# Moving five groups of SBUF tiles to different start bytes modulo 512 in a TensorE-bound kernel

## The chip, the core and the metric

The kernel runs on one core of a Trainium2 chip. The time is the device time of one execution in microseconds (us), the median of three runs.

## What is computed

A decaying (retention-like) attention over 2 batches, 8 heads, 768 positions and head size 64 gives 1536 tokens of 512 features. Two feed-forward layers follow, and they are most of the work:

```python
def _moe_ref(x, w_in, w_out):            # 512 -> 2048 -> 512
    h = x @ w_in
    g = np.where(h >= 1, h, np.where(h <= -1, 0.0, (h + 1) ** 2 / 4))
    return g @ w_out
def _moe2_ref(x, w_gate, w_val, w_out):  # 512 -> 1536 -> 512
    gate = 1.0 / (1.0 + np.exp(-(x @ w_gate)))
    return (gate * (x @ w_val)) @ w_out
```

The weights arrive as 64-bit floats, all else in 32 bits.

## The kernel before

Every large product is made of single-pass matmuls (type `float32r`) on a high and a low part of each operand: high times high, low times high and high times low, summed in PSUM. A matmul has a stationary operand of 128 by 128, which a weight load (LDWEIGHTS, row PEld of the profile) puts into the array, and a moving operand of 128 by 512, which is then streamed past it. Each matmul has its own weight load. All of this is on TensorE, in the order in which the code issues it.

- Up to some 66 us the attention runs, in small fp32 matmuls, with the first products of the first layer between them.
- `hidden` (lines 211 to 213) multiplies a slice of weights `w` (stationary) by the tokens `xh`, `xl` (moving), 12 matmuls per call. It serves the whole first layer and a third of the second.
- `project` (line 265) is the second product of each layer, 12 matmuls per call. In the first layer the weights are stationary and the activations `gh`, `gl` moving; in the second layer the activations are stationary and the weights moving. (The trace lists the operands of line 265 with the moving one first.)
- `product` (line 387), called seven times by `pair` with 6 matmuls each, serves two thirds of the second layer's first products by a scheme with fewer multiplications: the stationary operand is `w` or a sum or difference of weights (the "forms", tiles `s`), the moving one is `xh`, `xl` or a sum or difference of tokens (the "token forms", `xth`, `xtl`).

VectorE (DVE), ScalarE (ACT) and GpSimd (POOL) convert the weights to high and low parts (lines 99 to 120), apply the activation functions and add finished PSUM sums into `part` (line 287). The DMA queue of SyncE brings the weights.

The tiles of a pool lie one behind the other in each partition of SBUF, each rounded up to 32 bytes, and the pools follow each other in the order in which they are opened: `wp` (weights), `rawp`, `tp`, `xp` (tokens), `gp` (activations), `acp` (`half` and `part0`), then `late` (`part1`, `part2`, token forms) and `fp` (forms). The tiles of these pools are multiples of 512 bytes, except `half`, one number of 4 bytes. A stationary slice is 512 bytes of a partition and begins at a multiple of 512 bytes within its tile, and a moving operand is 2048 bytes and does so too. So all operands of one group have the same start byte modulo 512.

Of the kernel before, what the change touches and what calls it, by code (L numbers as in the profile page):

```python
# [7 lines left out]
F32 = mybir.dt.float32  # L8
# [9 lines left out]
P = 128  # L18
# [21 lines left out]
def fused_kernel(ctx: ExitStack, tc: tile.TileContext, qkv, qd, cst, w1, w2, out):  # L40
# [3 lines left out]
    wp = ctx.enter_context(tc.tile_pool(name="wp", bufs=NWP))  # L44
    rawp = ctx.enter_context(tc.tile_pool(name="rawp", bufs=NRAW))
    tp = ctx.enter_context(tc.tile_pool(name="tp", bufs=2))
    xp = ctx.enter_context(tc.tile_pool(name="xp", bufs=1))
    psx = ctx.enter_context(ExitStack())
    banks = {None: psx.enter_context(tc.tile_pool(name="ps", bufs=8, space=PSUM))}
    gp = ctx.enter_context(tc.tile_pool(name="gp", bufs=4))  # L50
    acp = ctx.enter_context(tc.tile_pool(name="acp", bufs=1))

# [161 lines left out]
        return h  # L214


    half = acp.tile([P, 1], F32, name="half")
    part = {0: acp.tile([P, 4, 512], F32, name="part0")}
    seq = []
    n0 = 0  # L220
# [597 lines left out]


    late = ctx.enter_context(tc.tile_pool(name="late", bufs=1, reuse_waits="tile"))  # L820
    fp = ctx.enter_context(tc.tile_pool(name="fp", bufs=4, reuse_waits="tile"))
    for t in range(1, NTT):
        part[t] = late.tile([P, 4, 512], F32, name=f"part{t}")
# [72 lines left out]
```

## Time and profile before

| | |
|---|---|
| median of three runs | 612.15 us |
| the three runs | 609.75, 612.15, 612.18 us |
| span of the profiled execution, first to last instruction | 608.4 us |
| median less span (what lies around it) | 3.75 us |
| PE busy | 596.9 us, 98% of the span |
| PEld, DVE, ACT, POOL busy | 80%, 71%, 53%, 18% |

Matmuls are pipelined: one begins before the one before it has left the array, so the duration of a row and the distance between two starts (called the pitch below) are two numbers. A busy share of 98% says only that matmuls follow each other without gaps.

### The profile page before, as it was taken

To read this page: it belongs to the slowest core of one execution; us is meant where nothing else is said; L and a number is where in the kernel's file an instruction comes from. 1 tells how busy PE (TensorE), PEld (TensorE's weight loads), DVE (VectorE), ACT (ScalarE), POOL (GpSimd) and SP (SyncE) were. 2 spreads that over 40 slices of the span, in tenths; PEclk is the share of its full clock that TensorE was granted. 3 is DMA by queue.
4 is the path that set the end of the run, shared out by engine and by line. 5 is a ranking of instruction groups with operands and counts; after the bars stand their busy time and mean duration, and the time that the engine had idled before them with its cause. 6 is when DMAs were issued, how large, how long until landed. Compare 5 with 4: busy or idle time off the path is not lost.

```text
span 608.4 us, 7945 instructions
## 1 busy us (share of the span) xinstructions
PE 596.9 (98%) x3016; PEld 487.4 (80%) x3016; DVE 429.4 (71%) x701; ACT 323.1 (53%) x585; POOL 110.9 (18%) x116
## 2 busy tenths in 40 slices
PE   7999999999999999999989999999999999999997
PEld 4887888888888888888868888878888888878885
DVE  7788853677587477467685887699697698594444
ACT  6798663675465466366563556555554554441220
POOL 4379500000000000000000231351241141150000
PEclk9999999999999999999999999999999999999999
DMA  8993420123122022123120223213123123000013
GB/s 298 397 330 132 139 69 2 71 103 103 36 79 95 0 90 85 34 70 103 36 69 0 70 70 103 70 52 123 34 70 103 36 69 105 0 1 0 1 69 138
DMA packets 15813, 52.58 MB, mean 86 GB/s; under 512 B 1688, under 2 KB 2976, under 8 KB 15776
## 3 DMA queue, kind: packets, MB, share of 16 engines
q1 hardware_dynamic: 15760, 52.08, 24.8%
q8 instruction: 23, 0.38, 0.3%
q14 instruction: 14, 0.11, 0.1%
q10 hardware_dynamic: 16, 0.01, 0.0%
HBM read 48.92 MB, written 3.15 MB: 86 GB/s over the span
## 4 chain that ended last, share of the span: by engine, by line
PE 87%; DVE 5%; DMA 4%; ACT 1%; issue 1%; POOL 1%; SPq 0%; DVEq 0%; ACTq 0%; POOLq 0%
PE a L265 35%; PE p L387 15%; PE h L211 11%; PE h L212 11%; PE h L213 11%; DMA u<-in_qkv 2%; DMA raw<-in_w 2%; PE x L748 1%; PE s L666 1%; PE x L739 1%; DVE wr L110 1%; DVE w L120 1%; DVE part L287 1%; DVE gl L433 1%; POOL wr L135 1%
## 5 line engine op out<-in xcount | busy, mean ns | idle before, releaser
L211 PE MATMUL h<-xh,w 128*128 128x512 f32 x320 | 125.9, 393 | 2.2 <-DVE part L287 2.2
L212 PE MATMUL h<-xh,w 128*128 128x512 f32 x320 | 125.2, 391 | 0.0
L213 PE MATMUL h<-xl,w 128*128 128x512 f32 x320 | 125.0, 391 | 0.0
L265 PE MATMUL a<-gh,w 128*128 128x512 f32 x384 | 118.5, 390 | 0.0
L265 PE MATMUL a<-w,gh 128*128 128x512 f32 x288 | 89.0, 390 | 0.1
L246 DVE SCALAR_TENSOR_TENSOR r<-r,h 128x512 f32<-128x512 f32 x48 | 33.0, 687 | 75.1 <-ACT r L242 75.1
L265 PEld LDWEIGHTS a<-gh,w 128*128 128x128 f32 x384 | 72.0, 188 | 15.1 <-POOL w L120 0.3
L241 ACT ACTIVATE r<-h,half 128x512 f32<-128x512 f32 x48 | 33.1, 689 | 89.5 <-PE h L213 89.5
L135 POOL TENSOR_TENSOR wr<-wr 128x256 f32<-128x256 f32 x20 | 16.9, 845 | 347.7 <-DVE w L120 346.9
L287 DVE TENSOR_TENSOR part<-part,a 128x512 f32<-128x512 f32 x108 | 68.1, 681 | 10.2 <-PE a L265 10.2
L265 PE MATMUL a<-gl,w 128*128 128x512 f32 x192 | 74.8, 390 | 0.5 <-DVE gl L234 0.5
L211 PEld LDWEIGHTS h<-xh,w 128*128 128x128 f32 x320 | 60.4, 189 | 15.6 <-DVE part L287 2.7
L213 PEld LDWEIGHTS h<-xl,w 128*128 128x128 f32 x320 | 60.3, 189 | 12.7
L212 PEld LDWEIGHTS h<-xh,w 128*128 128x128 f32 x320 | 60.5, 189 | 12.5
L265 PEld LDWEIGHTS a<-w,gh 128*128 128x128 f32 x288 | 54.0, 188 | 12.0 <-DVE part L287 0.6
L265 PE MATMUL a<-w,gl 128*128 128x512 f32 x144 | 56.6, 393 | 0.4 <-DVE gl L433 0.4
L110 DVE SCALAR_TENSOR_TENSOR wr<-raw,wr 128x512 uint32<-128x512 uint32 x68 | 51.5, 758 | 2.3
L116 ACT ACTIVATE w<-wr 128x512 fp32r<-128x512 f32 x68 | 42.3, 622 | 17.8 <-DVE wr L112 14.9
L233 ACT ACTIVATE gh<-r 128x512 fp32r<-128x512 f32 x64 | 40.0, 625 | 20.9 <-DVE r L246 11.5
L120 DVE TENSOR_TENSOR w<-wr,w 128x512 fp32r<-128x512 f32 x61 | 48.9, 801 | 1.8 <-ACT w L116 1.8
L234 DVE TENSOR_TENSOR gl<-r,gh 128x512 fp32r<-128x512 f32 x64 | 44.6, 696 | 7.7 <-ACT gh L233 7.7
L112 DVE CUSTOM_DVE_ANT_0 wr<-wr,wc 128x1024 uint16<-128x1024 uint16 x60 | 45.2, 753 | 2.7
(92 smaller groups left out, 877.0 us busy)
## 6 DMA issues: line engine op xcount, KB each, us to landing
raw<-in_w SPq DMA_DIRECT2D x68, 512.0 KB, 3.5
u<-in_qkv SPq DMA_DIRECT2D x12, 768.0 KB, 8.2
u<-in_qkv SPq DMA_DIRECT2D x8, 384.0 KB, 5.7
out<-part SPq DMA_DIRECT2D x12, 256.0 KB, 2.0
DT<-pd SPq DMA_DIRECT2D x1, 256.0 KB, 6.5
qp<-pd SPq DMA_DIRECT2D x2, 96.0 KB, 4.4
DT<-pd SPq DMA_DIRECT2D x1, 128.0 KB
cs<-in_cst SPq DMA_DIRECT2D x1, 98.0 KB, 1.9
```

Source lines behind the costliest of these rows:

```text
L110: dve.scalar_tensor_tensor(out=ru, in0=hi, scalar=0x80000000, in1=ru, op0=ALU.bitwise_and, op1=ALU.bitwise_or)
L112: eng.tensor_tensor(out=ri, in0=ri, in1=c, op=ALU.add)
L116: act.activation(ws[i][:, 0], tmps[i][1], AF.Copy)
L120: eng.tensor_tensor(out=ws[i][:, 1], in0=r, in1=ws[i][:, 0].bitcast(F32), op=ALU.subtract)
L211: pe.matmul(h, lhsT=wh, rhs=xh[:, k, tt], start=(k == 0), stop=False)
L212: pe.matmul(h, lhsT=wl, rhs=xh[:, k, tt], start=False, stop=False)
L213: pe.matmul(h, lhsT=wh, rhs=xl[:, k, tt], start=False, stop=(k == NP - 1))
L233: act.activation(gh, g, AF.Copy)
L234: dve.tensor_tensor(out=gl, in0=g, in1=gh.bitcast(F32), op=ALU.subtract)
L265: pe.matmul(accs[j], lhsT=a, rhs=b_, start=(first and m == 0), stop=(last and m == 2))
L287: dve.tensor_tensor(out=o, in0=o, in1=accs[j], op=ALU.add)
L387: pe.matmul(o, lhsT=a, rhs=b_, start=(start and k == 0 and m == 0), stop=(k == HK - 1 and m == 2), skip_group_check=True)
```

## The change

Four paddings are put into the order of the pools. Three are pools with one tile that nobody writes or reads (64, 64 and 416 bytes); the fourth is a wider tile for `half`, 288 bytes instead of 4, of which the same one number is used. No instruction is added, removed or moved; only addresses change.

```diff
+    def shift(name, n):
+        pool_ = ctx.enter_context(tc.tile_pool(name=name, bufs=1))
+        pool_.tile([P, n // 4], F32, name=f"{name}_")
+
+    shift("shx", 64)
     xp = ctx.enter_context(tc.tile_pool(name="xp", bufs=1))
...
+    shift("shg", 64)
     gp = ctx.enter_context(tc.tile_pool(name="gp", bufs=4))
...
-    half = acp.tile([P, 1], F32, name="half")
+    half = acp.tile([P, 72], F32, name="half")[:, 0:1]
...
     late = ctx.enter_context(tc.tile_pool(name="late", bufs=1, reuse_waits="tile"))
+    shift("shf", 416)
     fp = ctx.enter_context(tc.tile_pool(name="fp", bufs=4, reuse_waits="tile"))
```

Start bytes modulo 512, counted from those of the weights:

| group | before | after |
|---|---|---|
| weights `w` | 0 | 0 |
| tokens `xh`, `xl` | 0 | 64 |
| activations `gh`, `gl` | 0 | 128 |
| token forms `xth`, `xtl` | 32 | 416 |
| forms `s` | 32 | 320 |

Distance of the moving operand's start byte from the stationary operand's, modulo 512:

| product | matmuls | before | after |
|---|---|---|---|
| tokens on weights, lines 211 to 213 | 960 | 0 | 64 |
| activations on weights, line 265, first layer | 576 | 0 | 128 |
| weights on activations, line 265, second layer | 432 | 0 | 384 |
| tokens on weights, line 387 | 120 | 0 | 64 |
| token forms on forms, line 387 | 120 | 0 | 96 |
| tokens on forms, line 387 | 120 | 480 | 256 |
| token forms on weights, line 387 | 60 | 32 | 416 |

## Rows read from the trace of the kernel before

**Rows 1.** The page: busy time of the engines, and slices of the span.
```profile
PE 596.9 (98%) x3016; PEld 487.4 (80%) x3016; DVE 429.4 (71%) x701; ACT 323.1 (53%) x585; POOL 110.9 (18%) x116
...
PE   7999999999999999999989999999999999999997
...
PEclk9999999999999999999999999999999999999999
```

**Rows 2.** The chain that ended last: start us, us, engine, tile, line, instructions.
```profile
406.04 5.44 PE a L265 x24
411.48 6.88 PE p L387 x30
...
423.81 9.70 PE p L387 x42
```

**Rows 3.** Timeline of PE, first layer: start us, us, line, operands, instructions merged.
```profile
200.04 0.62 PE L265 MATMUL a<-gh,w 128*128 128x512 f32 x2
...
202.08 0.39 PE L211 MATMUL h<-xh,w 128*128 128x512 f32 x1
```

**Rows 4.** Timeline of PE, second layer, products on forms.
```profile
377.66 0.63 PE L387 MATMUL p<-xh,s 128*128 128x512 f32 x2
...
379.06 0.62 PE L387 MATMUL p<-xh,w 128*128 128x512 f32 x2
```

**Rows 5.** Matmuls of line 387 by operands: duration ns, lowest/median/highest.
```profile
L387 PE MATMUL p<-xh,w x80: 387/389/395, 363.9 to 569.8; 128*128 128x512 f32 x80
...
L387 PE MATMUL p<-xth,s x80: 387/389/398, 366.7 to 572.5; 128*128 128x512 f32 x80
...
L387 PE MATMUL p<-xh,s x80: 392/396/404, 369.4 to 579.4; 128*128 128x512 f32 x80
...
L387 PE MATMUL p<-xl,s x40: 395/396/397, 369.9 to 579.7; 128*128 128x512 f32 x40
...
L387 PE MATMUL p<-xth,w x40: 393/395/399, 376.3 to 578.0; 128*128 128x512 f32 x40
...
L387 PE MATMUL p<-xtl,w x20: 389/393/397, 376.7 to 578.3; 128*128 128x512 f32 x20
```

**Rows 6.** Groups of PE's instructions by form: count, busy us, mean ns, idle before.
```profile
L211 PE MATMUL h<-xh,w 128*128 128x512 f32 x320 | 125.9, 393 | 2.2 <-DVE part L287 2.2
...
L265 PE MATMUL a<-gh,w 128*128 128x512 f32 x384 | 118.5, 390 | 0.0
L265 PE MATMUL a<-w,gh 128*128 128x512 f32 x288 | 89.0, 390 | 0.1
L265 PE MATMUL a<-gl,w 128*128 128x512 f32 x192 | 74.8, 390 | 0.5 <-DVE gl L234 0.5
L265 PE MATMUL a<-w,gl 128*128 128x512 f32 x144 | 56.6, 393 | 0.4 <-DVE gl L433 0.4
```

**Rows 7.** Stages: us, busy us (instructions) of PE, PEld, DVE, ACT, POOL, granted clock, DMA.
```profile
319.00:322.00 3.00, 3.00 (x8) 2.32 (x9) 2.96 (x4) 0.00 (x0) 0.00 (x0) 0.50 0.00 1
...
400.00:450.00 50.00, 50.00 (x220) 40.85 (x219) 42.80 (x63) 27.09 (x49) 16.88 (x17) 1.00 0.23 74
```

**Rows 8.** Timeline of PE around the low clock.
```profile
318.80 0.79 PE L211 MATMUL h<-xh,w 128*128 128x512 f32 x1 [2.24 <-DVE part L287]
319.40 0.63 PE L212 MATMUL h<-xh,w 128*128 128x512 f32 x1
...
321.96 0.42 PE L212 MATMUL h<-xh,w 128*128 128x512 f32 x1
322.21 0.39 PE L213 MATMUL h<-xl,w 128*128 128x512 f32 x1
322.44 0.39 PE L211 MATMUL h<-xh,w 128*128 128x512 f32 x1
...
323.59 0.39 PE L213 MATMUL h<-xl,w 128*128 128x512 f32 x1
```

**Rows 9.** Timeline of the weight loads in the same place.
```profile
322.21 0.19 PEld L211 LDWEIGHTS h<-xh,w 128*128 128x128 f32 x1
322.44 0.19 PEld L212 LDWEIGHTS h<-xh,w 128*128 128x128 f32 x1
```

## The prediction

> **What bounds the kernel now.** The page comes first [rows 1]. PE is busy for 98% of the span, nearly every slice shows a 9, and the granted clock is full in all 40. The other engines stand between 18% and 71%. So 596.9 of 608.4 us pass with one matmul behind the other, and only two things can move the time: how many matmuls there are, which doesn't change, and the pitch, the distance from one start to the next. The busy share can't tell the pitch, for overlapping matmuls are busy all the time however far apart they start; so I read the pitch from the chain and the timeline.
>
> The chain that ended last has stretches of PE alone [rows 2]: 24 matmuls of line 265 in 5.44 us are 226.7 ns each. The timeline of the first layer has nine matmuls from 200.04 to 202.08 us, again 226.7 ns [rows 3]. All of these have operands that start at the same byte modulo 512 (distance 0 in the table above).
>
> The second place to look is line 387, the only line where two distances occur before the change. Its 42 matmuls at 423.81 us take 9.70 us [rows 2]. By the order of the code these are the last two products of one pair and the first five of the next: 24 with distance 0 and 18 with operands 32 bytes apart. If the 24 take 226.7 ns, 4.26 us are left for the 18, which is 236.7 ns, 10.0 more. The 30 at 411.48 us (24 at 0, six at 32) leave 1.44 us for the six, 13.3 ns more each. Alone, six matmuls of tokens on forms go from 377.66 to 379.06 us, 233.3 ns each, 6.6 more [rows 4]; the difference to 10.0 is what their neighbours lose behind them. The durations say the same by operands [rows 5]: medians of 389 ns for tokens on weights and for high token forms on forms (both at 0), 396 and 396 for tokens on forms, 395 and 393 for token forms on weights (all 32 apart). The same line, instruction and shape, with another start byte, is about 6.5 ns longer. So start bytes do matter here, and nearly 2400 matmuls carry them.
>
> Third, is there anything to gain? Around 320 us PE ran at a granted clock of 0.50, its lower level of 1.2 GHz, after 2.24 us of idleness before a matmul that waited for VectorE [rows 7, 8]. From 319.40 to 321.96 us six matmuls have a pitch of 426.7 ns. That is 512 columns at 1.2 GHz, with nothing on top. At 2.4 GHz the same would be 213.3 ns, but 226.7 is what the rows show. So 13.3 ns of each matmul are no streaming of columns. They appear only when the moving operand is read at its full rate, while the weight load of the next matmul is read beside it: at 322.21 us the load for the matmul of 322.44 starts in the same moment as the matmul before it [rows 8, 9]. I read the 13.3 ns as the two reads of SBUF getting into each other's way, and the 32-byte rows as the same thing at another distance.
>
> **The change part by part.** Nothing is issued, waited for or moved; queues, DMAs and waits stay as they are, and the paddings, 800 bytes per partition in all, are never written. The wider `half` is read through the same one column. So the whole change is the price of seven new distances: 64, 96, 128, 256, 384 and 416 instead of 0, 32 and 480.
>
> The counts come from the code and the groups agree with them [rows 5, 6]: 960 matmuls in `hidden`, 1008 in `project`, 420 in `product`; 2388 in all. Of these 2208 are at distance 0 now and 180 are 32 bytes apart.
>
> No row has one of the new distances, so their price is bounded from both sides:
> - Least: no interference, 213.3 ns. 2208 matmuls gain 13.3 ns (29.4 us) and 180 gain 23.3 (4.2 us): 33.6 us, a time of 578.5 us.
> - Most: all new distances cost what 32 bytes cost. 2208 matmuls lose 6.5 ns by the durations (14.4 us) or 10.0 by the chain (22.1 us): 626.5 to 634 us.
>
> The nearest rows in bytes are the 32-byte ones, and they are slower. I still don't take them. Distances 0, 32 and 480 all let both reads start within 32 bytes, eight columns, of each other. They sample one neighbourhood, and inside it the price jumps by half of the 13.3 ns, so it is no slow function of distance. From 64 to 256 bytes apart the reads start 16 to 64 columns apart, and the cost of their meeting can be a quite different one. I take the middle between the floor of 213.3 and the 226.7 of now, 220 ns, and this choice is the weakest step.
>
> Step 1: 2208 x 6.67 ns = 14.7 us gained. Step 2: 180 x (10.0 + 6.67) ns = 3.0 us gained. Step 3, given back: the pitch needs some matmuls to settle after a disturbance. Behind the low clock, all at distance 0, six matmuls from 322.21 to 323.59 us need 230 ns each [rows 8], 20 ns more in all than the settled pitch. Before the change almost all blocks have the same distance and nothing disturbs them; after it the distance changes from block to block. There are 80 blocks of `hidden`, 84 of `project` and 70 of `product`: 234 x 0.02 = 4.7 us lost at most, and I take all of it. In sum -14.7 - 3.0 + 4.7 = -13.0 us. The span of 608.4 becomes 595.4 us; with the 3.75 us by which the median lies above the span, the time is 599 us.
>
> What covers the rest of the kernel holds: the fullest stage of VectorE, 400 to 450 us, has 42.8 us of work in 50 [rows 7], 88% if PE takes 3% less. At the floor it would be 91%, and waits of PE for VectorE such as the one at 318.80 us (2.24 us) could then come back a few times.
>
> **Rivals.**
> - *Faster, the forecast* (chance 0.66): a pitch between 213 and 225 ns, 578 to 609 us, likeliest 599.
> - *Slower: any distance but 0 is a bad one* (0.20). The mechanism is in the rows: at distance 0 the two reads fall into a settled rhythm of 226.7 ns, and 32 bytes off, to either side, they don't [rows 4, 5]. If that rhythm needs equal start bytes, the change takes it from all 2208 matmuls: 627 us, 634 with the price of the chain. It speaks for this that both rows measured off 0 are slower and none is faster; against it, that 32 bytes either way are the smallest steps off 0 there are here. It decides as soon as the mean pitch over all blocks is above 228.1 ns (0.5% of 612 us is 3.06 us, or 1.3 ns on each of 2388 matmuls).
> - *No difference* (0.14): what counts repeats after fewer bytes than 512, say 64. Then 64, 128, 256 and 384 are the same as 0, and 96 and 416 the same as 32: the 1968 matmuls of `hidden` and `project` stay at 226.7 ns, in `product` 120 get worse and 120 get better, and the time stays at 612 us. For it speaks that the 24 matmuls of line 265, whose stationary slices lie 512 bytes apart, all have one pitch [rows 2], so some repetition there is; that it is shorter than 512, no row says.
>
> The Trainium skill has a rule against any effect at all: in "TensorE: Matmul & The Clock Gate", "Step-by-step: what each phase is for", TensorE has two independent read ports, and loading the next weights takes no SBUF bandwidth from the running matmul. By it the time stays at 612 us, as in the rival just named. The durations of 389 and 396 ns for the same line [rows 5] don't agree with it, so I leave that rival at 0.14. The same page, under "Wait — 56ns, not 53.3ns?", gives 215.7 ns as the pitch of 512 columns at the full clock, 11 ns less than the 226.7 of these rows; by it an undisturbed stream would be an estimated 584 us (2208 x 11.0 + 180 x 21.0 ns = 28.1 us).
>
> **How the numbers follow.** The measurement of this kernel can tell about 0.5%, 3 us, from no change. The forecast's case holds 0.66 and lies below 609 us, "no difference" holds 0.14 between 609 and 615, and the slower case 0.20 above. So faster is 0.66, same 0.14, slower 0.20. The range reaches from the floor, 578 us, to the end of "no difference", 615 us, and leaves out the slower case, two in ten. The likeliest time is 599 us.
>
> **What the profile after would show.** If step 1 is right, 24 matmuls of line 265 in the chain take about 5.28 us instead of 5.44, and the median durations at lines 211, 213 and 265 fall from 389 to some 382 ns. If step 2 is right, the four medians of 393 to 396 ns at line 387 fall to the others. If step 3 is right, the first matmuls of a block have other durations than the last. PE's busy share stays near 98% in every case: it is the pitch that tells. I am wrong if the medians at lines 211 and 265 rise to 395 or so (the rhythm is lost everywhere) or stay at 389 (it repeats within 512 bytes); or if the pitch falls but PE starts to wait for VectorE between 400 and 550 us.

## The result and the profile after

The changed kernel takes 618.97 us (median of four runs, 618.66 to 619.87); the kernel before took 611.54 us on the same chip (median of four, 609.75 to 612.18). The two medians differ by 7.4 us; the ratio of the two kernels' runs is 1.0138 with a 95% interval of 1.0116 to 1.0161, which is 8.4 us (7.1 to 9.8): slower, clear of noise. The forecast was faster, 599 us. The profiled execution agrees: its span is 617.1 us, 8.7 more than before.

The page after, busy time of the engines, answers to [rows 1]:

```profile
PE 607.6 (98%) x3016; PEld 489.8 (79%) x3016; DVE 429.4 (70%) x701; ACT 323.1 (52%) x585; POOL 111.1 (18%) x116
```

DVE and ACT are busy for exactly as long as before, and PE is still at 98%. Nothing new waits. PE does the same 3016 matmuls and is busy 10.7 us longer. Of these, 1.3 us lie in the first 15 us (12.17 us busy, 10.90 before), where the granted clock was 0.89 in this execution and 1.00 in the one before. The version with all groups at one start byte, below, has 0.89 there too, so this part doesn't come from the change.

The chain that ended last (start us, us, engine, tile, line, instructions; the lines are six higher than before, so line 271 is `project` and 393 `product`) answers to [rows 2]:

```profile
377.09 5.60 PE a L271 x24
382.68 9.72 PE p L393 x42
```

24 matmuls of `project` take 5.60 us, 233.3 ns each, where it was 226.7. The 42 of `product` take 9.72 us, where it was 9.70.

The timeline of PE in the first layer answers to [rows 3]:

```profile
201.70 0.64 PE L271 MATMUL a<-gh,w 128*128 128x512 f32 x2
...
204.49 0.40 PE L217 MATMUL h<-xh,w 128*128 128x512 f32 x1
...
207.25 0.40 PE L271 MATMUL a<-gh,w 128*128 128x512 f32 x1
```

A block of activations on weights lasts 2.79 us, 232.5 ns a matmul, and a block of tokens on weights 2.76 us, 230.0 ns.

The matmuls by line and operands (duration in ns, lowest/median/highest) answer to [rows 5] and, for lines 217 to 219 and 271, to the 389 ns that the prediction named:

```profile
L217 PE MATMUL h<-xh,w x320: 388/394/760, 39.4 to 601.3; 128*128 128x512 f32 x160
L218 PE MATMUL h<-xh,w x320: 388/388/628, 39.8 to 601.5; 128*128 128x512 f32 x160
L219 PE MATMUL h<-xl,w x320: 388/392/628, 40.0 to 601.7; 128*128 128x512 f32 x160
...
L271 PE MATMUL a<-gh,w x384: 390/393/475, 65.6 to 321.3; 128*128 128x512 f32 x192
...
L393 PE MATMUL p<-xth,s x80: 392/394/399, 372.7 to 580.8; 128*128 128x512 f32 x80
L393 PE MATMUL p<-xh,s x80: 387/393/398, 375.5 to 587.7; 128*128 128x512 f32 x80
```

No median has fallen below the 388 or 389 of an undisturbed matmul. Those that were at 389 have risen by 3 to 5 ns, but for line 218. Tokens on forms, at 396 before, have fallen to 393 and 394. The three lines of `hidden` have three medians: the pitch no longer repeats from one matmul to the next but every three.

### The profile page after: what moved, and what is told of

Same layout as the page of the kernel before. It is cut to its first block, busy times and chain, and to the rows that moved or that the text cites. A ratio compares the mean times of both kernels' runs of the same rounds, so it can differ in the third digit from the quotient of the medians.

```text
span 617.1 us, 7945 instructions
## 1 busy us (share of the span) xinstructions
PE 607.6 (98%) x3016; PEld 489.8 (79%) x3016; DVE 429.4 (70%) x701; ACT 323.1 (52%) x585; POOL 111.1 (18%) x116
## 4 chain that ended last, share of the span: by engine, by line
PE 94%; DVE 3%; ACT 1%; POOL 1%; issue 0%; DMA 0%; DVEq 0%; POOLq 0%; ACTq 0%
PE a L271 36%; PE p L393 15%; PE h L217 12%; PE h L219 12%; PE h L218 12%; PE x L754 2%; PE s L672 2%; PE x L745 2%; PE uu L687 1%; POOL wr L141 1%; DVE part L293 1%; DVE dm L609 0%; DVE gl L439 0%; ACT xh L303 0%; DMA cs<-in_cst 0%
## 5 line engine op out<-in xcount | busy, mean ns | idle before, releaser
L271 PE MATMUL a<-gh,w 128*128 128x512 f32 x384 | 120.6, 395 | 0.0
L271 PE MATMUL a<-w,gh 128*128 128x512 f32 x288 | 90.5, 395 | 0.0
L271 PEld LDWEIGHTS a<-w,gh 128*128 128x128 f32 x288 | 54.0, 188 | 13.1 <-DVE part L293 0.4
```

The costliest lines, as they stand in the source:

```text
L271: pe.matmul(accs[j], lhsT=a, rhs=b_, start=(first and m == 0), stop=(last and m == 2))
```

## The experiments

Theory A, formed on the result, is the rival of the prediction: equal start bytes are needed for the settled pitch of 226.7 ns. Theory B: a constant distance costs nothing, and only changing from one distance to the next does. Theory C: distance can help, and these six were badly chosen.

**One kernel with all distances.** In place of the computation, 16 blocks of 48 matmuls:

```python
for b, (name, d, s, cols, every, d2) in enumerate(BLOCKS):   # d: 0, 32, ... 480; s and every are 0
    ...
    for i in range(N):                                       # N is 48, P is 128
        a = s // 4 + i % 4 * P
        at = s + (d2 if every and i // every % 2 else d)
        c = at // 4 + i // 4 % 2 * 512
        pe.matmul(o[0:cols], lhsT=w[:, a:a + cols], rhs=x[:, c:c + 512], ...)
```

> This kernel leaves out the whole computation: after a warm-up block it runs 16 blocks of 48 matmuls (128 by 128 on 128 by 512, each with its own weight load), in which the moving operand starts 0, 32, ... 480 bytes behind the stationary one. Theory A, equal start bytes are needed for the settled rhythm: the block at 0 has a pitch of 226.7 ns and all 15 others lie between 229 and 235. Theory B, a constant distance costs nothing and only the change from one distance to another does: all 16 blocks are within 1.5 ns of 226.7, with some first matmuls of each off. Theory C, the six distances of the change were badly chosen: at least one of the other blocks is at 222 ns or below.

The timeline of PE, one row per block (start us, us, tile; `da` is distance 0, `db` 32, and so on to `dp`, 480). The distance between two starts, divided by 48, is the pitch:

```profile
24.02 11.04 PE L57 MATMUL da<-x,w 128*128 128x512 f32 x48
34.90 11.37 PE L57 MATMUL db<-x,w 128*128 128x512 f32 x48
46.10 11.16 PE L57 MATMUL dc<-x,w 128*128 128x512 f32 x48
57.10 11.37 PE L57 MATMUL dd<-x,w 128*128 128x512 f32 x48
68.31 11.36 PE L57 MATMUL de<-x,w 128*128 128x512 f32 x48
...
113.13 11.05 PE L57 MATMUL di<-x,w 128*128 128x512 f32 x48
124.02 11.37 PE L57 MATMUL dj<-x,w 128*128 128x512 f32 x48
135.22 11.16 PE L57 MATMUL dk<-x,w 128*128 128x512 f32 x48
```

| distance, bytes | 0 | 32 | 64 | 96 | 128 | 160 | 192 | 224 | 256 | 288 | 320 |
|---|---|---|---|---|---|---|---|---|---|---|---|
| pitch, ns | 226.7 | 233.3 | 229.2 | 233.5 | 233.3 | 234.2 | 233.1 | 233.1 | 226.9 | 233.3 | 229.2 |

The five blocks behind repeat the row from 96 to 224 (the last one, with no start behind it, by its duration). So in steps of 32 bytes the pattern repeats after 256 bytes, not 512; within it 0 is the best distance, 64 the second, and the rest cost 6 to 8 ns. No distance gains. Theory A holds but for 256; C falls for steps of 32 bytes; B falls, since constant distances cost.

The prices add up to about the result: 960 matmuls from 0 to 64 (2.5 ns, 2.4 us), 576 from 0 to 128 and 432 from 0 to 384 (6.6 ns, 6.7 us), in `product` 120 from 0 to 64 (0.3 us) and 120 from 0 to 96 (0.8 us), 120 from 480 to 256, of which by the chain of before each cost 10.0 ns (-1.2 us), and 60 from 32 to 416, about the same. That is 9.0 us; 8.4 were measured by the ratio, 7.4 between the medians. The sum is borne out better than its terms: from start to start in the two traces (distances over 300 ns left out), the six groups of products cost 2.8 us (tokens on weights in `hidden`), 5.6 (`project`), 0.1, 0.5, -0.3 and 0.1 us (`product`, in the order above), 8.8 in all, against 8.7 between the two spans. The 120 matmuls at 256 go from 233.9 to 231.2 ns only, and `project` in the second layer had 228.0 ns before (227.1 with all groups at one start byte, below), not 226.7.

**Finer steps**, the same kernel with 16 other distances.

> The sweep (the whole computation left out) at distances of 4, 8, 12, 16, 20, 24, 28, 36, 40, 48, 56, 60, 224, 240, 248 and 252 bytes. The theory that 0 modulo 256 is the best distance expects no block settled below 226.7 ns. A block below 226 would be a distance with which the kernel could be made faster.

Timeline of PE; `da` is a distance of 4 bytes, `de` 20, `dg` 28, `dl` 60:

```profile
23.03 11.52 PE L57 MATMUL da<-x,w 128*128 128x512 f32 x48
34.38 11.36 PE L57 MATMUL db<-x,w 128*128 128x512 f32 x48
...
67.71 11.68 PE L57 MATMUL de<-x,w 128*128 128x512 f32 x48
79.22 11.37 PE L57 MATMUL df<-x,w 128*128 128x512 f32 x48
90.44 11.09 PE L57 MATMUL dg<-x,w 128*128 128x512 f32 x48
101.36 11.45 PE L57 MATMUL dh<-x,w 128*128 128x512 f32 x48
...
146.21 11.09 PE L57 MATMUL dl<-x,w 128*128 128x512 f32 x48
157.14 11.36 PE L57 MATMUL dm<-x,w 128*128 128x512 f32 x48
```

4 bytes cost 236.5 ns, 20 bytes 239.8, the worst of all; 28 and 60 bytes, each 4 short of a multiple of 32, come out at 227.5 and 227.7, while 56 has 232.5. None of the 31 distances in both sweeps lies below 226.7 ns. The price is no smooth function of distance, so a neighbour's row says nothing about the next one. A further kernel of blocks, below, repeats 4, 8 and 16 bytes on another chip within 0.2 ns. But at 496 bytes, which is 240 modulo 256, it has 236.0 ns where 240 has 233.3: the repetition after 256 bytes is shown for steps of 32, not for every finer one.

**All groups at one start byte.** The padding of `half` alone, now 512 bytes, takes away the 32 bytes between the pools of before:

```diff
-    half = acp.tile([P, 1], F32, name="half")
+    half = acp.tile([P, 128], F32, name="half")[:, 0:1]
```

> The kernel before with half padded to 512 bytes, so that all five groups start at the same byte modulo 512. Theory A: the 180 matmuls that were 32 bytes apart fall to 226.7 ns and nothing settles any more; by the chain of before that is 10 ns each, 1.8 us, so about 609.7 us, 0.3% below before, and in the trace all medians at line 387 are 389 ns. Theory B expects the same, since all switching between distances goes. If start bytes had nothing to do with it, no difference to before.

608.63 us against 610.23 on the same chip: ratio 0.9976, interval 0.9964 to 0.9989 (12 and 17 runs). This version is faster than both kernels. Its medians at line 387, and its chain at the places of [rows 2]:

```profile
L387 PE MATMUL p<-xth,s x80: 389/389/389, 366.8 to 571.4; 128*128 128x512 f32 x80
L387 PE MATMUL p<-xh,s x80: 387/389/441, 369.6 to 578.2; 128*128 128x512 f32 x80
```
```profile
411.53 6.80 PE p L387 x30
418.33 5.44 PE a L265 x24
423.77 9.52 PE p L387 x42
```

The 42 matmuls fall from 9.70 to 9.52 us, 226.7 ns each, and the 30 from 6.88 to 6.80 us. What the prediction read from the 32-byte rows, 1.8 us in all, is confirmed (1.6 by the medians, 0.7 to 2.2 by the interval).

**All 256 bytes apart.** If the pattern repeats after 256 bytes in the kernel too, other start bytes must be free:

```diff
...
+    shift("shx", 256)
     xp = ctx.enter_context(tc.tile_pool(name="xp", bufs=1))
...
+    half = acp.tile([P, 128], F32, name="half")[:, 0:1]
...
+    shift("shf", 256)
     fp = ctx.enter_context(tc.tile_pool(name="fp", bufs=4, reuse_waits="tile"))
```

> Tokens, activations and token forms 256 bytes behind the weights and forms, modulo 512: every product at distance 256. The sweep repeats after 256 bytes (226.8 ns at 256 as at 0), so the time is that of all_at_zero, 608.6 us within 1 us, although the operands no longer start at the same byte modulo 512. If the sweep's blocks of 48 equal matmuls don't stand for the kernel, it lies with tokens_at_64 near 615.

608.36 us, ratio to before 0.998 (0.9965 to 0.9995): the same as all at 0. So it is not moving the groups that costs, but by how much.

**One part at a time.** The tokens alone at 64 (paddings of 64, 448 and 512 bytes), and the activations alone at 128 (128 and 384 bytes), all else at 0:

> All groups at 0, the tokens alone at 64: 1080 matmuls at distance 64 and 120 at 64 (tokens on forms), 1188 at 0. In the changed kernel the pitch of lines 217 to 219 cycles through 226, 229 and 232 ns, 229.0 in the mean. Theory A: 1200 x 2.3 = 2.8 us above all_at_zero plus settling behind each change of distance, together 3 to 6 us, so 613 to 616. Theory B: the settling alone, 2 to 4 us.

> All groups at 0, the activations alone at 128: the 576 matmuls of line 265 in the first layer at distance 128 and its 432 in the second at 384, the rest at 0. By the sweep both cost 233.3 ns, 6.6 more than 0: 1008 x 6.6 = 6.7 us above all_at_zero (608.6), 615.3, and settling on top, up to 4 us: 615 to 619. If only changes of distance cost, the 4 us alone: at most 613.

614.83 us (ratio 1.0083, 1.0064 to 1.0102) and 614.86 us (1.0079, 1.0055 to 1.0103). Against the 608.63 and 608.36 us of the versions with all at 0 modulo 256, which ran beside them, these are 6.2 and 6.5 us more; the distances alone explain 3.0 (1200 x 2.5 ns) and 6.7 (1008 x 6.6 ns). For the activations that fits. For the tokens half of it is missing, and the chain shows where it is: activations on weights, which are at distance 0 here, take 2.77 us for 12, 230.8 ns, though nothing about them was changed:

```profile
134.08 2.77 PE a L271 x12
```

All 36 such blocks between 100 and 300 us take these 2.77 us, and only their last two matmuls are back at 227 ns. With the activations at 128 it is the blocks of tokens on weights that are at 0; they are back after three matmuls and take 2.74 us, 227.9 ns each. So a block can suffer from the distance of the block before it, and how much depends on the distances.

**Constant distances in the kernel.** Tokens, activations and token forms together at 64, or together at 128. (At 64, the second layer's weights on activations come to lie at 448, which is 192 modulo 256, so only the first layer is constant; at 128 everything is.)

```diff
...
+    shift("shx", 64)      # or 128
...
+    half = acp.tile([P, 128], F32, name="half")[:, 0:1]
...
+    shift("shf", 448)     # or 384
```

> Tokens, activations and token forms 64 bytes behind weights and forms: 64 everywhere but for line 265 in the second layer, where the weights move and the distance is 448, by the sweep the same as 192 (233.2 ns). In the first layer nothing switches: by the sweep 229 ns for its 1152 matmuls. With tokens_at_64 half of them are at 0, and the mean was 230.1. If switching costs on its own, the first layer (100 to 300 us) is now faster than in tokens_at_64, 229.0 to 229.2 ns a matmul; if only the distances count, it is slower than 227.9, the mean of 226.7 and 229.1, in both, and not faster here. The whole: 1956 x 2.4 + 432 x 6.5 = 7.5 us above 608.5, 616, and up to 2 us of settling.

> Every product at distance 128 (or 384, the same by the sweep), nothing switches between blocks. The sweep gives 233.3 ns, the columns run 232.1 to 232.4: 2388 x 5.7 to 6.6 = 13.6 to 15.8 us above 608.5, so 622 to 624, slower than the change. If the change's loss came from switching alone, it is near 608.5.

615.09 us (ratio 1.0080, 1.0061 to 1.0098) and 620.92 us (1.0174, 1.0149 to 1.0200). All at 128 is slower than the change although nothing switches: the distance costs by itself. (It misses the expected 622 to 624 us by one, as 128 costs less in the kernel than in the sweep.) The first layer separates the two costs. How many matmuls PE has in the same 200 us (first figure in brackets) for all at zero, tokens at 64, all at 64 and all at 128, then for activations at 128 and the changed kernel, in this order:

```profile
100.00:300.00 200.00, 200.00 (x884) 165.62 (x883) 136.18 (x225) 116.19 (x197) 0.00 (x0) 1.00 0.20 69
```
```profile
100.00:300.00 200.00, 200.00 (x869) 162.85 (x868) 134.42 (x222) 113.26 (x192) 0.00 (x0) 1.00 0.20 69
```
```profile
100.00:300.00 200.00, 200.00 (x876) 164.09 (x875) 134.41 (x222) 114.61 (x194) 0.00 (x0) 1.00 0.22 69
```
```profile
100.00:300.00 200.00, 200.00 (x862) 162.15 (x861) 132.82 (x220) 112.96 (x192) 0.00 (x0) 1.00 0.22 69
```
```profile
100.00:300.00 200.00, 200.00 (x870) 163.02 (x869) 134.05 (x222) 113.80 (x193) 0.00 (x0) 1.00 0.22 69
```
```profile
100.00:300.00 200.00, 200.00 (x866) 162.66 (x865) 133.77 (x222) 113.35 (x192) 0.00 (x0) 1.00 0.21 69
```

Scaled from 884 at 226.7 ns, tokens at 64 has 230.6 ns, all at 64 has 228.8 and all at 128 has 232.5. With twice as many matmuls off 0, all at 64 is faster in this stage than tokens at 64. So switching between distances costs on its own, as theory B said, next to the distance itself. How much depends on the pair. Half of the matmuls of this stage are tokens on weights and half activations on weights; against the mean of the two constant distances, switching between 0 and 64 costs 2.9 ns a matmul (230.6 against 227.7), but between 0 and 128 (230.3 against 229.6) and, in the changed kernel, between 64 and 128 (231.4 against 230.6) only 0.7 to 0.8.

**What the excess is made of.** Three kernels of blocks, as in the sweep.

> This kernel leaves out the whole computation: blocks of 48 matmuls as in the sweep. At distance 0 the stationary operand has 128, 96, 64 and 32 columns: if the 13.3 ns above 213.3 are the weight load's reads in the way of the moving operand's, the pitch falls with the columns, to some 223, 220 and 217 ns; if they are a fixed cost of a matmul, it stays at 226.7. At distance 64 with 64 and 32 columns: the first reading expects less than the 229 of 128 columns, the second 229. Both operands 32 and 64 bytes later: 226.7 if only the distance counts. Distances 0 and 64, and 64 and 128, by turns every 12 matmuls: theory A expects the mean of the two blocks of constant distance or up to 3 ns more, theory B at least 3 ns more than either. Distances 4, 8, 16, 496 and 508: no theory has a number; 226.7 up to 12 or 16 bytes would say that a line of some bytes counts.

> Blocks of 48 matmuls (the whole computation left out) with 512, 448, 384, 320 and 288 moving columns, at distance 0 and at 128. If the excess over the streaming time is paid for each matmul, the pitches at 0 are the columns at 2.4 GHz plus 13.3 ns: 226.7, 200.0, 173.3, 146.7 and 133.3. If it is paid for each column streamed (1.026 ns for 64 columns would be 1.67): 226.7, 198.3, 170.0, 141.7 and 127.5. At 128 the same with 20 ns in the place of 13.3. Last four blocks with operands of 2 bytes at distances 0, 32, 64 and 128 bytes: if the excess comes from reading 4 bytes per column at the full clock, all four have one pitch between 213 and 217 ns; if it belongs to any matmul, 226.7 at 0 and some 233 at 32.

> Blocks of 48 matmuls, the whole computation left out. The start bytes change by turns from matmul to matmul, between 0 and 64, 0 and 128, 0 and 32. In oa, ob and oc each moving operand starts at the byte of its own stationary operand and off that of the next; in xa, xb and xc at the byte of the next and off its own. If what counts is the weight load that runs beside the matmul, the next one's, then xa, xb and xc settle at 226.7 ns and oa, ob and oc lie near the constant distances (229 to 233). If the matmul's own stationary operand counts, it is the other way round. If neither is at 226.7, the start bytes matter in a way that a pair of operands doesn't describe. Constant distances 64, 448, 128 and 32 as controls: 229, 233, 232 to 233 and 233 ns.

The first one's timeline: `ca` to `cd` have 128, 96, 64 and 32 stationary columns at distance 0; `alt` and `alu` change every 12 matmuls between 0 and 64, and between 64 and 128:

```profile
23.63 11.04 PE L56 MATMUL ca<-x,w 128*128 128x512 f32 x48
34.52 11.21 PE L56 MATMUL cb<-x,w 128*96 128x512 f32 x48
45.56 11.20 PE L56 MATMUL cc<-x,w 128*64 128x512 f32 x48
56.60 11.29 PE L56 MATMUL cd<-x,w 128*32 128x512 f32 x48
67.72 11.13 PE L56 MATMUL ce<-x,w 128*64 128x512 f32 x48
...
111.61 11.19 PE L56 MATMUL alt<-x,w 128*128 128x512 f32 x48
122.64 11.26 PE L56 MATMUL alu<-x,w 128*128 128x512 f32 x48
133.73 11.52 PE L56 MATMUL fa<-x,w 128*128 128x512 f32 x48
```

Fewer stationary columns don't lower the pitch: 226.9, 230.0, 230.0 and 231.7 ns, although the weight load gets shorter, from 188 to 161, 134 and 108 ns. At distance 64 it is 228.5 ns with 64 columns and 231.3 with 32, against 229.2 with all. That goes against the reading that the 13.3 ns are the weight load's reads. Both operands 64 bytes later make 227.3 ns (from 100.70 to 111.61 us); the first seven matmuls settle and the rest have 226.7, so the distance counts and not the address. Taking turns between 0 and 64 costs 229.8 ns, 1.9 more than the mean of 226.7 and 229.2; between 64 and 128 it costs 231.0, no more than the mean of the sweep's 229.2 and 233.3.

The second one's, with 512, 448, 384, 320 moving columns at distance 0 (`na` to `nd`) and 512 columns of 2-byte operands at distances 0 and 32 (`ba`, `bb`; the trace has 47 of their 48 matmuls):

```profile
23.65 11.04 PE L58 MATMUL na<-x,w 128*128 128x512 f32 x48
34.53 9.89 PE L58 MATMUL nb<-x,w 128*128 128x448 f32 x48
44.26 8.48 PE L58 MATMUL nc<-x,w 128*128 128x384 f32 x48
52.58 7.19 PE L58 MATMUL nd<-x,w 128*128 128x320 f32 x48
59.61 6.49 PE L58 MATMUL ne<-x,w 128*128 128x288 f32 x48
...
119.14 10.52 PE L58 MATMUL bb<-xb,wb 128*128 128x512 bf16 x47
129.50 10.52 PE L58 MATMUL bc<-xb,wb 128*128 128x512 bf16 x47
```

The pitches are 226.7, 202.7, 173.3 and 146.5 ns, and 131.7 with 288 columns (`ne`). Less the columns at 2.4 GHz that leaves 13.3, 16.0, 13.3, 13.1 and 11.7 ns: at distance 0 the excess is paid for each matmul and hardly by the column. What a distance of 128 adds is another matter: the same widths have 232.5, 204.0, 176.0, 146.7 and 133.3 ns there, 5.8, 1.3, 2.7, 0.2 and 1.7 more. Expected were 6.7 at every width, so the prices of the sweep are those of 512 columns. Operands of 2 bytes have 215.8 ns, 2.5 ns of excess, and the blocks at 32, 64 and 128 bytes have no other pitch. Their weight loads last 98 ns in place of 188, so this doesn't tell which of the two reads counts. The Trainium skill, "TensorE: Matmul & The Clock Gate", "Wait — 56ns, not 53.3ns?", gives 215.7 ns for 512 columns; these 2-byte blocks agree with it, the 4-byte ones of this kernel don't.

At the low clock a distance of 64 costs nothing either: after the same wait as before the change, with a granted clock of 0.50, six matmuls of the changed kernel, now at distance 64, have 426.7 ns, as at distance 0 before [rows 8]:

```profile
324.65 0.63 PE L218 MATMUL h<-xh,w 128*128 128x512 f32 x1
...
327.21 0.57 PE L218 MATMUL h<-xh,w 128*128 128x512 f32 x1
```

So the effect was seen only with 4-byte operands at the full clock.

The third kernel was to tell whether the matmul's own stationary operand counts or the next one's, which is loaded beside it. Its answer is neither: with 0 and 64 by turns 231.7 and 233.1 ns, with 0 and 128 by turns 228.3 and 230.0, with 0 and 32 by turns 231.9 and 230.6. No block of turns comes to 226.7. And its control at a constant 64 settled at 233.3 ns, where the sweep and the kernel had 229 (timeline of PE, `xa` one of the turns of 0 and 64, `zb` the constant 64):

```profile
44.76 11.36 PE L50 MATMUL xa<-x,w 128*128 128x512 f32 x48
55.95 11.36 PE L50 MATMUL zb<-x,w 128*128 128x512 f32 x48
67.15 11.36 PE L50 MATMUL zc<-x,w 128*128 128x512 f32 x48
```

One distance can thus settle in more than one way. The two blocks at 64 differ in what ran before them and in the chip, and no run separates these. At 128 the chip isn't needed: in the sweep the matmuls alternate between about 229 and 238 ns, 233.3 in the mean; in the first kernel of this section, on the same chip, those at 128 behind others at 64 go from 228 to 241 ns and back, as a constant 128 does on the other two chips (232.1 and 232.5 ns in the mean). There what ran before is enough to make the difference. Whole blocks (128 stationary and 512 moving columns of 4 bytes) at a constant distance 0 settled at 226.7 in every run.

## Why the prediction was wrong

- **What bounds the kernel: right.** The pitch alone moved the time; PE's share stayed at 98%, and the other engines' work didn't change.
- **Start bytes matter, and 32 bytes cost 6.5 to 10 ns: right.** The sweep has 233.3 ns at 32, and taking the 32 bytes away gave 1.6 us.
- **The floor of 213.3 ns as something to gain by distance: wrong.** The rows of the low clock were read rightly, but the excess was put down to two reads in each other's way. Fewer stationary columns don't lower it, and it is the same for 384 columns as for 512. So the rows bore no promise that distance could take it away, and none of the 31 does.
- **The step that failed is the choice of 220 ns for the new distances**, the middle between floor and now, against the only rows off 0, which were slower. Measured were 230.0 ns for the blocks that went to 64 and 232.5 for those that went to 128. Its reason was that 0, 32 and 480 sample one neighbourhood and far distances could be quite different. They are different, 64 from 128 above all, but none is better: 0 is a point by itself, it returns at 256, and everything else that was tried costs from 0.8 ns (28 bytes) to 13.1 (20 bytes). Step 1 forecast 14.7 us gained; the 2208 matmuls lost some 9 to 10.
- **Step 2, 3.0 us gained at the 180 matmuls: some 0.3.** Token forms on weights, at 416 now, have durations of 394 ns where they had 393 to 395. Tokens on forms, at 256 now, should have been free. Their pitch fell only from 233.9 to 231.2 ns, with medians of 393 and 394; their blocks of six stand between blocks at other distances, where by the block of 2.77 us above ten matmuls can be disturbed.
- **Step 3, settling: real, but not the same for every change.** It put 20 ns on each block. A block at 0 behind one at 64 loses 50 ns (12 times 4.1), a price that the change doesn't pay in its first layer; between 64 and 128 it is 0.7 to 0.8 ns a matmul, some 9 ns a block.
- **The rival "slower" was right that other distances lose the pitch of 226.7 ns, but for 256, at 0.20.** Its price was too high, 627 to 634 us, since it gave every distance the cost of 32 bytes and 64 costs only 2.5 ns. The point from which it decides, 228.1 ns, was passed: 230.0 and 232.5 ns in the two kinds of blocks of the first layer.
- **The rival "no difference" had the right idea and the wrong length:** the pattern repeats within 512 bytes, after 256. None of the change's distances but one is a multiple of it.
- **The range** ended at 615 us because it left the slower case out; by the rows off 0 that case had the better claim, and the range should have held it.
- **A slip without weight:** the prediction speaks of seven new distances; seven products change, and they have the six distances that it lists.

What stays open: why a 4-byte matmul pays 13.3 ns at distance 0 and up to 26.5 at 20 bytes, which pair of reads sets it, and why a distance costs less with fewer moving columns.

## What to carry to other kernels

Where a kernel is bound by back-to-back matmuls on 4-byte operands, read the pitch and not the busy share, and keep stationary and moving operands at the same start byte modulo 256; a constant of 4 bytes in front of a pool cost 0.2% here, and paddings meant to keep groups apart 1.4%. Also keep the distance the same from block to block, since a change of distance can disturb the blocks behind it (2.9 ns a matmul between 0 and 64, under 1 ns between 0 and 128). When only two distances can be read from a trace and the one off the present value is slower, that row is the estimate. A small kernel that tries all distances shows in one run which of them cost; their exact prices in a kernel differ by a nanosecond or more, with what runs before.

## What the runs showed of the hardware that was not expected

Where a block settles to one pitch for every matmul, it is 226.7, 230.0, 233.3 or, at 20 bytes, 240.0 ns, in steps of 3.3 ns. Other distances settle into cycles, with means in between: at 64 bytes 226, 229 and 232 ns in turn. Behind other distances a block of 48 at distance 0 came back to 226.7 ns after five to seven matmuls, and blocks of 12 behind 64 bytes only with their last two; the same 64 bytes settled once at 229 and once at 233.3 ns.
